# Weight bits routed through PSUM, and a planner that counts a shared port both ways, in a fused attention and feed-forward kernel

## The chip, the cores and the metric

The kernel runs on one core of a Trainium2 chip. The metric is the device time of one execution in microseconds. Five engines matter: TensorE (PE; its weight loads are listed apart as PEld), VectorE (DVE), ScalarE (ACT), GpSimd (POOL), and SyncE (SP), which issues the transfers. DVE and ACT reach both memories on the chip, SBUF and PSUM; PE writes to PSUM; POOL works in SBUF in this kernel.

## The reference

Attention over 2 x 8 heads with 1152 keys of 64 elements and queries averaged in pairs (576 of them), and then two feed-forward layers, on the 1152 x 512 result. The weights come as 64-bit floats.

```python
def _attn_ref(q, k, v):
    B, H, S, D = q.shape                       # 2, 8, 1152, 64
    q_pool = q.reshape(B, H, S // 2, 2, D).mean(axis=3)
    scores = (1 / np.sqrt(D)) * np.matmul(q_pool, k.transpose(0, 1, 3, 2))
    scores = scores - np.max(scores, axis=-1, keepdims=True)
    attn = np.exp(scores)
    attn = attn / (np.sum(attn, axis=-1, keepdims=True) + 1e-09)
    return np.matmul(attn, v)

def _moe_ref(x, w_in, w_out):                  # 1152 x 512, d_ff 2048
    h = x @ w_in
    g = np.where(h >= 1, h, np.where(h <= -1, 0.0, (h + 1) ** 2 / 4))
    return g @ w_out

def _moe2_ref(x, w_in, w_out):
    h = x @ w_in
    return (h / (1.0 + np.exp(-h))) @ w_out
```

## The kernel before

**Arithmetic.** Every operand of a large matmul is split into a high part in a short format (fp32r) and a low part, the rest. `lo_of` (line 135) computes the low part on POOL, in a few places on DVE. A product is then two or three matmuls.

**Attention.** The 16 heads run one after the other and overlap. `inputs(h)` loads q, k and v, splits and transposes k (`khl`, evacuated to `kk` at line 459) and q (`split_q` at line 470, evacuated to `qm` at lines 484 and 488). `scores(h, t)` multiplies a tile of 128 queries with the keys into three banks, which DVE evacuates with their least value (line 562); ACT takes the exponential (line 575). `values(h)` transposes the result in nine chunks (line 610), evacuates each into the two parts `thl` (`split`: either ACT at 588 and DVE at 589, or ACT at 593 and POOL at 594 and 135), and multiplies with v (line 618). The last 64 queries of two heads are done together in `tails`: DVE adds the halves into `ztail` (line 666), multiplies it with the inverse sums (line 670), and PE transposes it into place (line 675). `finish` scales the rows of a pair of heads (line 720).

**Feed-forward layers.** Each layer has four groups of 512 hidden columns, numbered 0 to 7 over both. A step is one group, one of three blocks of 384 tokens and one of four slices of 128 hidden columns: `gemm1` (line 155), the activation (168 to 184), `gemm2` (200, 202), and `keep` (212, 214), which adds to the sum in SBUF.

**Weights.** A group has two kinds of weights, w_in ("i") and w_out ("o"), each in four quarters. A quarter is loaded as 64-bit words (line 97) and made into 32-bit floats by `weight_tasks`: `size` takes the absolute value of the upper words on ACT (102), then four steps on DVE, `clamp` (105), `shift` (109), `sign` (113) and `rest` (117), each with 128 x 512 elements in SBUF, of which `sign` and `rest` read two tensors. ACT then writes the high part (125) and POOL the low part (135). Group 0 is done during attention, its w_in spread over the heads, its w_out after the last heads have been prepared; groups 1 to 7 are done from the opening of the feed-forward stage on (`weights`).

**PSUM.** Of the eight banks, six ("b") rotate over the scores, the transposes and, later, the sums of the layers; two ("y") hold the product with v. A bank is free again when the last step that names it is done.

**Order.** Nothing is scheduled by hand. Every step is an `Op` with a target time, the engines it may run on, the time that it occupies the engine and the time until its result is there, the steps it follows, and the buffers it uses. `plan_out` simulates the engines: again and again it takes the step that can start first, and among equals the one with the least target. The resulting order is the order of each engine's queue; on the chip an engine takes its queue in order and waits for semaphores. A step marked `both` is one that, on DVE, needs the port to SBUF that DVE and POOL share; the plan starts it only when no POOL step is running:

```python
if o.both and e == "DVE" and pool_until[0] <= s < pool_until[1]:
    s = pool_until[1]
...
if e == "POOL":
    pool_until = (s, s + lat)
```

Marked so are the four DVE steps of every weight quarter, the scaling of `ztail`, the scaling in `finish` where it falls on DVE, and the preparation of heads 0 and 1, which may run on DVE or on POOL (`first`).

Of the kernel before, what the change touches and what calls it, by code (L numbers as in the profile page):

```python
# [10 lines left out]
U32 = mybir.dt.uint32  # L11
AF = mybir.ActivationFunctionType
ALU = mybir.AluOpType
# [5 lines left out]
def fused_kernel(  # L19
# [11 lines left out]
    nc = tc.nc  # L31
# [16 lines left out]
    RAWS = 4  # L48
# [13 lines left out]
    LEAST = 2.0**-15  # L62
# [14 lines left out]
    def weight_tasks(idx, kind, pools, RAWS):  # L77
# [6 lines left out]
        def quarter(c):  # L84
# [19 lines left out]
            def clamp():  # L104
                nc.vector.tensor_scalar(st["w"], st["w"], LEAST, MOST, ALU.max, ALU.min)

            def shift():
                wi = st["w"].bitcast(U32)
                nc.vector.tensor_scalar(wi, wi, 3, 0x3FFFFFF8, ALU.logical_shift_left, ALU.bitwise_and)

            def sign():
                wi = st["w"].bitcast(U32)
                nc.vector.scalar_tensor_tensor(wi, st["top"], 0xC0000000, wi, ALU.bitwise_and, ALU.bitwise_or)  # L113

            def rest():
                wi = st["w"].bitcast(U32)
                nc.vector.scalar_tensor_tensor(wi, st["low"], 29, wi, ALU.logical_shift_right, ALU.bitwise_or)
# [144 lines left out]
    def plan_out():  # L262
# [21 lines left out]
        while len(made) < len(ops):  # L284
            best = None
            for e in engines:
                found = []
                for o, k, t in ready[e].values():
                    s = max(t, free[e])
                    for b in o.bufs:  # L290
                        if b.slot is None:
                            have = open_slots[b.group]
                            if b.want is not None:
                                have = [x for x in have if x[1] == b.want]
                            if not have:
                                s = None
                                break
                            s = max(s, min(have)[0] + (0.06 if e == "PE" else 0.04))
                    if s is None:
                        continue  # L300
                    if o.both and e == "DVE" and pool_until[0] <= s < pool_until[1]:
                        s = pool_until[1]
                    found.append((s, o.target, o, k))
# [13 lines left out]
            if e == "POOL":  # L317
                pool_until = (s, s + lat)
            made.append(o)
# [19 lines left out]
    with ExitStack() as at, ExitStack() as keys, ExitStack() as prep:  # L339
# [60 lines left out]
        def inputs(h):  # L400
# [33 lines left out]
            for part in [slice(3 * g, 3 * g + 3) for g in range(3)] if h == 0 else [slice(0, KC)] * 1:  # L434
# [5 lines left out]
                if first:  # L440
                    ways.insert(0, ("DVE", 0.1 + 0.6 * n, 0.18 + 0.6 * n, lo(nc.vector)))
                klo.append(op(t1 + 0.01, ways, [khi[-1]], [kr, kb], both=first))
# [31 lines left out]
            if first:  # L474
                ways.insert(0, ("DVE", 0.6, 0.69, lambda: split_q(nc.vector)))
            sq = op(t3, ways, [lq], [qr, qb], both=first)
# [157 lines left out]
        def tails(h):  # L634
# [35 lines left out]
            o2 = op(t1 + 0.4, ("DVE", 0.2, 0.28, lambda: nc.vector.tensor_scalar_mul(ztail, ztail, sums[key])), [o1, o_inv[key]], [zb], both=True)  # L670
# [98 lines left out]

        STAGES = (("ACT", 0.57, 0.672), ("DVE", 0.332, 0.42), ("DVE", 0.335, 0.427), ("DVE", 0.6, 0.69), ("DVE", 0.6, 0.69))  # L770
        w_last = [None]

        def weights(w, kind, times, deps):


            def get(n, m):
                if (w, kind) not in wsets:
# [4 lines left out]
                    wsets[w, kind] = weight_tasks(w, kind, pools, 1 if (w, kind) == (0, "i") else RAWS)  # L782
# [4 lines left out]
            made = []  # L787
            for n, t in enumerate(times):
                bufs = [Buf("w" if (w, kind) == (0, "i") else "raw"), *whole]
                prev = op(t - 5, ("SP", 2.0, 4.4, lambda n=n: get(n, 0)()), [*deps, w_last[0]], bufs)  # L790
                w_last[0] = prev
                for m, (e, occ, lat) in enumerate(STAGES):
                    prev = op(t + 0.3 * m, (e, occ, lat, lambda n=n, m=m: get(n, m + 1)()), [prev], bufs, both=e == "DVE")
# [114 lines left out]
```

## Time and profile before

| | us |
|---|---|
| median of 3 runs | 695.96 |
| lowest and highest of them | 695.18, 696.70 |
| the profiled execution, its own time | 693.9 |
| its span, first to last instruction | 692.1 |
| TensorE busy | 678.8 |
| VectorE busy | 547.1 |
| GpSimd busy | 431.2 |
| ScalarE busy | 413.7 |

The span is what the rows of the trace add up to; the profiled execution's own time is 1.8 us longer, and the median lies 2.1 us above that. The granted clock of TensorE is 1.00 of full speed in all stretches of the attention and feed-forward stages. A busy PE in this page is one whose pipeline holds a matmul: the rows of neighbouring matmuls overlap, so a stop shows as a gap between rows that is shorter than the time lost. The attention stage ends at about 290 us.

### The profile page before, as it was taken

The numbers are of one execution on the slowest core, as the hardware profiler recorded it, in microseconds if no ns is written. First come the engines' busy times: TensorE is split into PE (matmuls) and PEld (weight loads), VectorE is DVE, ScalarE is ACT, GpSimd is POOL, SyncE is SP. The second block draws the span as 40 slices with busy tenths as digits, with TensorE's granted clock in tenths as the row PEclk, the third lists the DMA queues.
The fourth block names the chain that finished last, engine by engine and source line by source line (L and its number), as shares of the span: only waits on it lengthen the run. The fifth ranks groups of instructions, "written<-read, shape, count | busy, mean of one in ns | idle before, by whom it ended". The sixth has DMA issues, their size and how long they took to land.

```text
span 692.1 us, 11265 instructions
## 1 busy us (share of the span) xinstructions
PE 678.8 (98%) x3959; PEld 627.4 (91%) x3959; DVE 547.1 (79%) x1205; ACT 413.7 (60%) x773; POOL 431.2 (62%) x406
## 2 busy tenths in 40 slices
PE   8999999999999998999999999999999999999997
PEld 6898989888989997899999999999898999999896
DVE  7889989898888889658999796897884894993223
ACT  7988997968797887545544444454554543442221
POOL 7959897969796757735654455478664554453221
PEclk9999999999999999999999999999999999999999
DMA  7332231222110032102332232122131221200012
GB/s 210 109 92 59 92 112 38 79 72 65 50 49 11 26 124 76 62 31 92 122 123 91 92 106 79 61 92 92 62 121 62 92 93 60 93 30 1 1 45 92
DMA packets 28489, 52.93 MB, mean 76 GB/s; under 512 B 4752, under 2 KB 13968, under 8 KB 28432
## 3 DMA queue, kind: packets, MB, share of 16 engines
q1 hardware_dynamic: 28432, 52.21, 23.6%
q8 instruction: 31, 0.51, 0.3%
q14 instruction: 26, 0.21, 0.1%
HBM read 49.81 MB, written 2.39 MB: 75 GB/s over the span
## 4 chain that ended last, share of the span: by engine, by line
PE 81%; DVE 8%; POOL 7%; issue 2%; ACT 1%; DMA 0%; SPq 0%; POOLq 0%; DVEq 0%; ACTq 0%
PE bank L155 27%; PE bank L200 14%; PE bank L202 14%; PE bank L555 9%; PE bank L618 7%; PE bank L610 6%; DVE p L562 2%; POOL thl L135 2%; PE bank L656 2%; POOL xl L135 1%; POOL thl L594 1%; DVE thl L589 1%; PE bank L454 1%; PE bank L647 1%; DVE wf L113 1%
## 5 line engine op out<-in xcount | busy, mean ns | idle before, releaser
L135 POOL TENSOR_TENSOR gl<-gf,gh 128x384 fp32r<-128x384 f32 x96 | 112.4, 1171 | 119.2 <-ACT gh L184 117.5
L155 PE MATMUL bank<-xh,whi 128*128 128x384 f32 x384 | 129.2, 337 | 0.0
L155 PE MATMUL bank<-xl,whi 128*128 128x384 f32 x384 | 129.2, 336 | 0.0
L155 PE MATMUL bank<-xh,wli 128*128 128x384 f32 x384 | 128.9, 336 | 0.0
L562 DVE TENSOR_SCALAR_CACHE_REDUCE p<-bank 128x384 f32<-128x384 f32 x192 | 101.3, 550 | 18.8 <-PE bank L555 17.5
L618 PE MATMUL bank<-thl,vhl 128*128 128x512 f32 x288 | 112.4, 433 | 2.8 <-DVE thl L589 1.5
L178 DVE TENSOR_TENSOR gf<-bank,gf 128x384 f32<-128x384 f32 x96 | 52.9, 551 | 61.6 <-ACT gf L170 57.7
L555 PE MATMUL bank<-kk,qm 128*128 128x384 f32 x384 | 95.3, 352 | 1.9 <-DVE thl L589 1.7
L610 PE MATMUL bank<-ident,p 128*128 128x128 f32 x576 | 85.3, 273 | 0.0
L135 POOL TENSOR_TENSOR thl<-pf,thl 128x512 fp32r<-128x512 f32 x64 | 83.1, 1298 | 3.3
L575 ACT ACTIVATE p<-p,low 128x1152 f32<-128x1152 f32 x64 | 81.0, 1266 | 5.7 <-DVE low L572 5.5
L184 ACT CAST gh<-gf 128x384 fp32r<-128x384 f32 x96 | 49.4, 514 | 53.1 <-DVE gf L178 52.0
L113 DVE SCALAR_TENSOR_TENSOR wf<-wr,wf 128x512 uint32<-128x512 uint32 x64 | 76.2, 1191 | 1.2
L610 PEld LDWEIGHTS bank<-ident,p 128*128 128x128 f32 x576 | 69.4, 140 | 7.8 <-DVE thl L589 0.3
L555 PEld LDWEIGHTS bank<-kk,qm 128*128 128x128 f32 x384 | 65.4, 189 | 10.7 <-DVE thl L589 3.3
L155 PEld LDWEIGHTS bank<-xl,whi 128*128 128x128 f32 x384 | 72.1, 188 | 2.1
L155 PEld LDWEIGHTS bank<-xh,whi 128*128 128x128 f32 x384 | 72.1, 188 | 2.0
L155 PEld LDWEIGHTS bank<-xh,wli 128*128 128x128 f32 x384 | 72.1, 188 | 0.0
L589 DVE TENSOR_TENSOR thl<-bank,thl 128x512 fp32r<-128x512 f32 (+1 forms) x104 | 66.8, 653 | 3.6 <-ACT thl L588 3.3
L588 ACT CAST thl<-bank 128x512 fp32r<-128x512 f32 (+1 forms) x104 | 57.1, 562 | 20.6 <-PE bank L610 16.7
L170 ACT ACTIVATE gf<-bank 128x384 f32<-128x384 f32 x48 | 23.6, 492 | 76.5 <-PE bank L155 73.2
L135 POOL TENSOR_TENSOR wli<-wf,whi 128x512 fp32r<-128x512 f32 x32 | 43.1, 1347 | 41.7 <-ACT whi L125 41.5
(90 smaller groups left out, 1537.7 us busy)
## 6 DMA issues: line engine op xcount, KB each, us to landing
wr<-in_moe_w_in_dram SPq DMA_DIRECT2D x32, 512.0 KB, 3.7
wr<-in_moe_w_out_dram SPq DMA_DIRECT2D x32, 512.0 KB, 3.3
kraw<-in_k_dram SPq DMA_DIRECT2D x16, 288.0 KB, 2.9
vraw<-in_v_dram SPq DMA_DIRECT2D x16, 288.0 KB, 2.8
qraw<-in_q_dram SPq DMA_DIRECT2D x16, 256.0 KB, 3.0
out_dram<-part SPq DMA_DIRECT2D x9, 256.0 KB, 2.0
rb<-row SPq DMA_DIRECT2D x16, 128.0 KB, 3.3
qtraw<-in_q_dram SPq DMA_DIRECT2D x16, 32.0 KB, 2.5
```

The costliest lines, as they stand in the source:

```text
L113: nc.vector.scalar_tensor_tensor(wi, st["top"], 0xC0000000, wi, ALU.bitwise_and, ALU.bitwise_or)
L135: eng.tensor_sub(out, whole, hi.bitcast(F32))
L155: nc.tensor.matmul(ps, lhsT=w[:, c, j * P : (j + 1) * P], rhs=a[:, c, ts_], start=(c == 0 and n == 0), stop=(c == ND - 1 and n == 2),)
L200: nc.tensor.matmul(ps[:, :TB], lhsT=w[:, j, m * P : (m + 1) * P], rhs=a, start=start, stop=stop)
L202: nc.tensor.matmul(ps, lhsT=a[:, m * P : (m + 1) * P], rhs=w[:, j, :], start=start, stop=stop)
L555: nc.tensor.matmul(ps, lhsT=qq[:, c0 : c0 + P], rhs=rhs, start=n == 0, stop=n == last)
L562: nc.vector.tensor_scalar(dst, ps, -1.0, None, ALU.mult, ALU.min, accum_out=mxs[key, t][:, j : j + 1])
L575: nc.scalar.activation(pt(), pt(), AF.Exp, bias=lows[key][:, tt : tt + 1], scale=-1.0, accum_out=sums[key][:, tt : tt + 1])
L588: o1 = op(target, ("ACT", 0.477 * f, 0.587 * f, lambda: nc.scalar.copy(th(), ps())), deps, [bank, tb])
L589: o2 = op(target + 0.3, ("DVE", 0.6 * f, 0.683 * f, lambda: nc.vector.tensor_sub(tl(), ps(), th().bitcast(F32))), [o1], [bank, tb])
L610: nc.tensor.transpose(banks[bank.slot][:, i * P : (i + 1) * P], ps_[p_of[h, i].slot][:, c * P : (c + 1) * P], ident)
L618: nc.tensor.matmul(banks[6 + yb.slot], lhsT=lhsT, rhs=thls[tb.slot][i], start=not count, stop=len(count) == 2 * KC - 1)
```

## The change

Four edits.

- For group 0 (`w` is 0), both kinds, `clamp` writes into a PSUM bank that the quarter holds (`via`), `shift` and `sign` work in that bank, and `rest` reads it and writes SBUF again. These four steps get the costs of `FAR`, 0.6 us each, are no longer marked `both`, and name one of the rotating banks. Groups 1 to 7 are done as before.
- The plan's rule for the port gets a margin of 0.1 us, and a second side: a marked step that starts on DVE keeps POOL from starting until 0.1 us before its end.
- The preparation of head 1 (low part of k, sum of q) may run on POOL alone; head 0 keeps both ways.
- `ztail` is scaled by ACT instead of DVE.

```diff
-    def weight_tasks(idx, kind, pools, RAWS):
+    def weight_tasks(idx, kind, pools, RAWS, via):
...
             def clamp():
-                nc.vector.tensor_scalar(st["w"], st["w"], LEAST, MOST, ALU.max, ALU.min)
+
+                st["x"] = via[c]() if c in via else st["w"]
+                nc.vector.tensor_scalar(st["x"], st["w"], LEAST, MOST, ALU.max, ALU.min)
 
             def shift():
-                wi = st["w"].bitcast(U32)
-                nc.vector.tensor_scalar(wi, wi, 3, 0x3FFFFFF8, ALU.logical_shift_left, ALU.bitwise_and)
+                xi = st["x"].bitcast(U32)
+                nc.vector.tensor_scalar(xi, xi, 3, 0x3FFFFFF8, ALU.logical_shift_left, ALU.bitwise_and)
 
             def sign():
-                wi = st["w"].bitcast(U32)
-                nc.vector.scalar_tensor_tensor(wi, st["top"], 0xC0000000, wi, ALU.bitwise_and, ALU.bitwise_or)
+                xi = st["x"].bitcast(U32)
+                nc.vector.scalar_tensor_tensor(xi, st["top"], 0xC0000000, xi, ALU.bitwise_and, ALU.bitwise_or)
 
             def rest():
-                wi = st["w"].bitcast(U32)
-                nc.vector.scalar_tensor_tensor(wi, st["low"], 29, wi, ALU.logical_shift_right, ALU.bitwise_or)
+                wi, xi = st["w"].bitcast(U32), st["x"].bitcast(U32)
+                nc.vector.scalar_tensor_tensor(wi, st["low"], 29, xi, ALU.logical_shift_right, ALU.bitwise_or)
...
-                    if o.both and e == "DVE" and pool_until[0] <= s < pool_until[1]:
+                    if o.both and e == "DVE" and pool_until[0] - 0.1 <= s < pool_until[1]:
                         s = pool_until[1]
...
             if e == "POOL":
                 pool_until = (s, s + lat)
+            elif o.both and e == "DVE":
+                free["POOL"] = max(free["POOL"], s + lat - 0.1)
...
-                if first:
+                if not h:
                     ways.insert(0, ("DVE", 0.1 + 0.6 * n, 0.18 + 0.6 * n, lo(nc.vector)))
-                klo.append(op(t1 + 0.01, ways, [khi[-1]], [kr, kb], both=first))
+                klo.append(op(t1 + 0.01, ways, [khi[-1]], [kr, kb], both=not h))
...
-            if first:
+            if not h:
                 ways.insert(0, ("DVE", 0.6, 0.69, lambda: split_q(nc.vector)))
-            sq = op(t3, ways, [lq], [qr, qb], both=first)
+            sq = op(t3, ways, [lq], [qr, qb], both=not h)
...
-            o2 = op(t1 + 0.4, ("DVE", 0.2, 0.28, lambda: nc.vector.tensor_scalar_mul(ztail, ztail, sums[key])), [o1, o_inv[key]], [zb], both=True)
+            o2 = op(t1 + 0.4, ("ACT", 0.17, 0.28, lambda: nc.scalar.mul(ztail, ztail, sums[key])), [o1, o_inv[key]], [zb])
...
+        FAR = (("ACT", 0.57, 0.672), *[("DVE", 0.6, 0.69)] * 4)
         STAGES = (("ACT", 0.57, 0.672), ("DVE", 0.332, 0.42), ("DVE", 0.335, 0.427), ("DVE", 0.6, 0.69), ("DVE", 0.6, 0.69))
...
             for n, t in enumerate(times):
                 bufs = [Buf("w" if (w, kind) == (0, "i") else "raw"), *whole]
+                bank = Buf("b")
+                if not w:
+                    via[n] = lambda bank=bank: banks[bank.slot]
                 prev = op(t - 5, ("SP", 2.0, 4.4, lambda n=n: get(n, 0)()), [*deps, w_last[0]], bufs)
                 w_last[0] = prev
-                for m, (e, occ, lat) in enumerate(STAGES):
-                    prev = op(t + 0.3 * m, (e, occ, lat, lambda n=n, m=m: get(n, m + 1)()), [prev], bufs, both=e == "DVE")
+                for m, (e, occ, lat) in enumerate(STAGES if w else FAR):
+                    more = bufs if w or not m else [*bufs, bank]
+                    prev = op(t + 0.3 * m, (e, occ, lat, lambda n=n, m=m: get(n, m + 1)()), [prev], more, both=e == "DVE" and w > 0)
```

## Rows read from the trace of the kernel before

**Rows 1.** Head of the page: span; busy time, share of the span, instructions.

```profile
span 692.1 us, 11265 instructions
PE 678.8 (98%) x3959; PEld 627.4 (91%) x3959; DVE 547.1 (79%) x1205; ACT 413.7 (60%) x773; POOL 431.2 (62%) x406
```

**Rows 2.** Busy us by stretch: PE, PEld, DVE, ACT, POOL; then clock, DMA share, GB/s.

```profile
160.00:250.00 90.00, 90.00 (x616) 82.52 (x615) 76.12 (x253) 76.02 (x138) 69.24 (x74) 1.00 0.18 49
250.00:291.00 41.00, 37.86 (x232) 33.69 (x231) 36.14 (x85) 28.89 (x54) 31.24 (x30) 1.00 0.27 84
```

**Rows 3.** Waits of PEld, 50 to 160 us: us in total, times, longest us.

```profile
PEld bank L555 <- DVE thl L589: 2.5, 2, 2.2
PEld bank L618 <- POOL thl L594: 2.2, 7, 0.5
...
PEld bank L454 <- DVE p L562: 1.1, 2, 0.9
```

**Rows 4.** Waits of PEld, 160 to 250 us, the only kind listed.

```profile
PEld bank L555 <- DVE thl L589: 0.9, 2, 0.4
```

**Rows 5.** Timeline, PE: start, us, what; in brackets PE's idle time before it.

```profile
148.92 0.45 PE L454 MATMUL bank<-ident_r,khl 128*128 128x128 f32 x3 [0.70 <-DVE p L562]
...
159.22 0.62 PE L555 MATMUL bank<-kk,qm 128*128 128x384 f32 x2 [1.72 <-DVE thl L589]
...
261.28 0.98 PE L555 MATMUL bank<-kk,qt 128*128 128x384 f32 x4 [0.58 <-DVE low L572]
...
266.97 0.43 PE L675 MATMUL bank<-jtail,ztail 128*128 128x64 f32 x2 [0.60 <-DVE ztail L670]
...
273.41 0.50 PE L618 MATMUL bank<-thl,vhl 128*128 128x512 f32 x1 [0.76 <-DVE thl L589]
```

**Rows 6.** Timeline, DVE and one of POOL, before those stops.

```profile
143.91 0.53 DVE L105 TENSOR_SCALAR wf<-wf 128x512 f32<-128x512 f32 x1
...
146.60 1.79 DVE L113 SCALAR_TENSOR_TENSOR wf<-wr,wf 128x512 uint32<-128x512 uint32 x1
...
156.47 1.54 POOL L720 TENSOR_TENSOR y<-y,rb 128x512 f32<-128x512 f32 x1 [0.18 <-DVE y L629]
156.49 2.07 DVE L117 SCALAR_TENSOR_TENSOR wf<-wr,wf 128x512 uint32<-128x512 uint32 x1
...
258.97 1.65 DVE L113 SCALAR_TENSOR_TENSOR wf<-wr,wf 128x512 uint32<-128x512 uint32 x1
...
265.57 1.34 DVE L670 TENSOR_SCALAR ztail<-ztail,sum 128x128 f32<-128x128 f32 x1
...
270.99 1.76 DVE L117 SCALAR_TENSOR_TENSOR wf<-wr,wf 128x512 uint32<-128x512 uint32 x1
```

**Rows 7.** Tile wf: ns min/median/max, first and last start in us, forms.

```profile
L105 DVE TENSOR_SCALAR wf<-wf x64: 394/422/1515, 58.5 to 620.6; 128x512 f32<-128x512 f32 x64
L109 DVE TENSOR_SCALAR wf<-wf x64: 409/590/1499, 62.6 to 621.0; 128x512 uint32<-128x512 uint32 x64
L113 DVE SCALAR_TENSOR_TENSOR wf<-wr,wf x64: 672/1344/1833, 64.3 to 621.8; 128x512 uint32<-128x512 uint32 x64
L117 DVE SCALAR_TENSOR_TENSOR wf<-wr,wf x64: 673/694/2070, 73.1 to 623.2; 128x512 uint32<-128x512 uint32 x64
```

**Rows 8.** Groups by form: count, busy us, mean ns of one, idle before.

```profile
L589 DVE TENSOR_TENSOR thl<-bank,thl 128x512 fp32r<-128x512 f32 x96 | 65.2, 684 | 3.6 <-ACT thl L588 3.3
...
L521 ACT ACTIVATE qt<-bank 128x128 fp32r<-128x128 f32 x8 | 2.2, 278 | 0.0
```

**Rows 9.** Waits of PEld, 300 to 690 us, both kinds listed.

```profile
PEld bank L200 <- DVE part L214: 1.3, 2, 1.1
PEld bank L202 <- POOL gl L135: 1.0, 1, 1.0
```

**Rows 10.** Timeline, POOL, at the start: the second head's q and k.

```profile
6.74 1.29 POOL L470 TENSOR_TENSOR qs<-qraw 128x512 f32<-128x512 f32 x1 [0.67 <-DMA qraw<-in_q_dram]
...
8.39 1.44 POOL L135 TENSOR_TENSOR khl<-kraw,khl 128x576 fp32r<-128x576 f32 x1
```

More of the change, by code (lines that the diff above doesn't have):

```diff
@@ L781, in get @@
                         pools = (nat, wpre) if kind == "i" else late_raws()
-                    wsets[w, kind] = weight_tasks(w, kind, pools, 1 if (w, kind) == (0, "i") else RAWS)
+                    wsets[w, kind] = weight_tasks(w, kind, pools, 1 if (w, kind) == (0, "i") else RAWS, via)
                 return wsets[w, kind][n][m]
@@ L786, in weights @@
             whole = [Buf("w" + kind)] if w else []
-            made = []
+            made, via = [], {}
             for n, t in enumerate(times):
                 bufs = [Buf("w" if (w, kind) == (0, "i") else "raw"), *whole]
+                bank = Buf("b")
+                if not w:
+                    via[n] = lambda bank=bank: banks[bank.slot]
                 prev = op(t - 5, ("SP", 2.0, 4.4, lambda n=n: get(n, 0)()), [*deps, w_last[0]], bufs)
                 w_last[0] = prev
-                for m, (e, occ, lat) in enumerate(STAGES):
-                    prev = op(t + 0.3 * m, (e, occ, lat, lambda n=n, m=m: get(n, m + 1)()), [prev], bufs, both=e == "DVE")
+                for m, (e, occ, lat) in enumerate(STAGES if w else FAR):
+                    more = bufs if w or not m else [*bufs, bank]
+                    prev = op(t + 0.3 * m, (e, occ, lat, lambda n=n, m=m: get(n, m + 1)()), [prev], more, both=e == "DVE" and w > 0)
                 prev = op(t + 2, ("ACT", 0.51, 0.61, lambda n=n: get(n, 7)()), [prev], bufs)
```

## The prediction
> **What bounds the kernel now.** I read the page first. TensorE (PE) is busy for 678.8 of 692.1 us [rows 1], so another engine costs time only where it makes PE stop, and the question is not how long VectorE (DVE) and GpSimd (POOL) work but which PE stops they cause. The sums by stretch come next: from 160 to 250 us, where no weight is converted, PE is busy for all of 90.00 us while DVE is busy for 76.12 of them; from 250 to 291 us, where the four quarters of the first w_out group are converted, PE is busy for 37.86 of 41.00 [rows 2]. The waits of the weight loads, which show a stop of PE a little earlier than its matmuls do, say the same: between 50 and 160 us, the stretch of the four quarters of the first w_in group, the three largest kinds shown sum to 2.5 + 2.2 + 1.1 = 5.8 us [rows 3]; the 90 us without weights have 0.9 us [rows 4]. So the first weight group is what makes the attention stage stop.
>
> The timeline shows how. Five stops of PE, 0.70, 1.72, 0.58, 0.60 and 0.76 us, sum to 4.36 us [rows 5]. Just before each stands one DVE instruction that reads and writes SBUF only and takes far longer than its kind can: L113 1.79 us, L117 2.07, L113 1.65, the scaling of ztail at L670 1.34, L117 1.76 [rows 6]. The shortest of the kind are 672 ns for L113 and 673 for L117 [rows 7]. The clearest case is at 156.49 us: L720 on POOL started 0.02 us earlier and ended at 158.01; L117 ended at 158.56 [rows 6], so it got about 0.55 us of work done after POOL had let go. Behind it on DVE stood the evacuation L589, and PE waited for that. The instructions of DVE with a PSUM operand are not held up this way: L589, 96 of them with POOL busy for most of the stage, means 684 ns [rows 8], against 672 for the undisturbed L113.
>
> **The change, part by part.**
>
> *Weight bits through PSUM.* In 8 quarters the four DVE steps get a PSUM operand, so each has at most one SBUF operand. What goes: the excess of the four L113 and L117 above is 1.79 - 0.67 = 1.12, 2.07 - 0.67 = 1.40, 1.65 - 0.67 = 0.98 and 1.76 - 0.67 = 1.09 us. A stop can't give back more than the excess that made it, so 0.70 + 1.40 + 0.58 + 0.76 = 3.4 us come back.
>
> What it adds on DVE: clamp and shift run at 394 and 409 ns at their shortest [rows 7]. Neither SBUF to PSUM nor PSUM to PSUM is in the trace. The ends are their present shortest time and the 684 ns of L589 [rows 8]; I take 684, the nearest row with a PSUM operand of 512 columns. That is 0.29 + 0.275 us more, and 0.01 for each of the other two: 0.58 us for a quarter, 4.7 us for eight. I cost it at nothing: DVE idles for 13.9 of 90 us in the stretch without weights [rows 2], and the excess removed is larger than what is added. If that cover is gone it is 4.7 us.
>
> [...]
>
> What it adds as a wait: clamp now waits for a free bank, and from clamp to the last step one of the six rotating banks is taken from PE. Behind a waiting clamp on DVE stand the evacuations L562 and L589, and PE waits for those. The four steps of the fourth quarter now stretch from 143.91 to 158.56 us, 14.7 us [rows 6]; a bank would be held as long if they stay as spread. What a bank less costs no row shows. Lower end 0 (a bank taken away can't help); upper end one stop for each quarter like the longest in the stretch without weights, 0.4 us [rows 4]: 3.2 us. I take 0.1 for each, 0.8 us, since that stretch runs with two waits in 90 us and so has room.
>
> *ztail scaled by ScalarE (ACT).* Eight instructions leave DVE. The held one cost the stop of 0.60 us [rows 5] out of an excess of 1.34 - 0.28 = 1.06, so 0.60 us comes back. On ACT it should take 278 ns, as L521 of 128x128 does [rows 8], 2.2 us in all; ACT is busy 76.02 of 90 us [rows 2], which covers it. It waits there for the sum's inverse and for L666; behind it stand an exponential or an evacuation, and PE waits for that. Price if the cover fails: 0.28 us each, 2.2 us.
>
> *POOL's side.* A POOL instruction also waits where DVE came first. The waits for L594 are 2.2 us, seven of them [rows 3]. Between 0 and 2.2 I take 0.5, since most are short and a matmul in flight hides part of each.
>
> *Second head on POOL alone.* Its split of q and low part of k already run on POOL, at 6.74 and 8.39 us [rows 10]. Taking DVE's way from them changes no step that was chosen: nothing, with the start of the kernel as it is.
>
> *The plan counts the port both ways.* The plan gives the order on each engine and nothing else; it is no wait on the chip. In attention, hardly any DVE step is left that is marked as needing the port: those of head 0 and the scaling in `finish`, where that falls on DVE. So the new rule acts mainly from 300 us on, on the weights of groups 1 to 7. There two kinds of waits of PE's weight loads are listed, 1.3 us for L214 and 1.0 for POOL's gl [rows 9]. A better order removes them (-2.3), a worse one doubles them (+2.3); nothing chooses between the two, so I take 0 and keep both for the range. From the first ztail on, every later choice of the plan may also fall otherwise; I put no sign to that.
>
> Sum: -3.4 - 0.6 - 0.5 + 0.8 = -3.7 us. The profiled execution took 693.9 us, 1.8 beyond its span; it would take 690.2. The median of the runs shown is 695.96, 2.1 higher; the same 3.7 us less makes 692.3.
>
> **The rivals.**
>
> A, the freed time is used up: the two slower steps and the bank leave DVE as late as before at half of the stops. For it: DVE idles for only 4.9 of 41 us from 250 to 291 [rows 2], and four quarters come close together there. Against it: the held time removed is larger than what is added. Half of 4.0 comes back, the bank costs 0.8: -1.2, 694.8 us.
>
> B, slower: banks run short. Each quarter keeps a bank for as long as its steps are spread, and PE, which runs ahead of DVE only as far as it has banks, stops once for each quarter by the mean of today's stops, 4.36 / 5 = 0.87 us: 8 x 0.87 = 7.0, less the 4.5 won, +2.5: 698.5 us. It decides from 4.5 / 8 = 0.56 us for each quarter. For it: 14.7 us of holding, and up to four quarters close together after 250 us, where the first steps of the feed-forward layer hold banks as well. Against it: the nearly stopless 90 us.
>
> C, the change doesn't do what it says: the forms that no row shows, SBUF to PSUM and PSUM to PSUM, are held by POOL all the same. Then only ztail's 0.6 comes back against 0.8 for the banks: 696.2 us. Against it: of the forms with PSUM that are there, none is held [rows 8].
>
> D, the reordered feed-forward layers win too: -3.7 - 2.3, 690.0 us.
>
> **How the numbers follow.** Forecast 0.52, A 0.19, B 0.16, C 0.05, D 0.08. The forecast's 692.3 is the likeliest and the number given. 0.2% is 1.4 us, about what a measurement of this kernel can tell from no change. Faster by more: the forecast and D, 0.60. Within: A and C, 0.24. Slower: B, 0.16. The range goes from 687.5 (4.0 back, with all of 2.2 and 2.3 on top: 8.5 less) to 697.5 (4.0 back, but 3.2 for the banks and 2.3 for the order: 1.5 more); it leaves out B, 0.16.
>
> **What would show it.** In the trace after: the four steps of the first eight quarters all near 0.68 us, whatever POOL does, and all of L562 and L589 behind them on time; PE idle before 250 us near what the 90 us without weights have; ztail on ACT at about 0.28 us; the second head's two POOL steps at 6.7 and 8.4 us as now; the weights of groups 1 to 7 still held at times. I am wrong if the steps are held in PSUM too (C), if weight loads wait for banks that a weight quarter holds (B), if PE stops behind DVE in new places of the same size (A), or if the stretch from 300 us on gains or loses more than 2.3 us.

## The result, and the profile after

The changed kernel takes 689.02 us (median of 4 runs, 688.70 to 689.87) against 695.73 for the kernel before beside it (4 runs, 695.18 to 696.70): 0.9904 of it, interval 0.9887 to 0.9921. It is 6.7 us faster; the forecast was 3.7 us and its range held the time. Profiled execution against profiled execution it is 693.9 to 689.0, 4.9 us; the other 1.8 us lie between the profiled executions and the medians (below, the clock). In the code all lines from the edit on stand 2 to 4 lines lower: `clamp`, `shift`, `sign`, `rest` are L107, L111, L115, L119; the evacuations L562 and L589 are now L566 and L593; the transposes L610 are L614, the product with v L618 is L622, and the ztail scaling L670 is L674.

The page of the kernel after, its head:

```profile
span 687.1 us, 11298 instructions
...
PE 678.8 (99%) x3959; PEld 627.0 (91%) x3959; DVE 524.7 (76%) x1191; ACT 418.0 (61%) x787; POOL 424.8 (62%) x406
```

Against [rows 1], TensorE (PE) has the same 678.8 us of work in a span that is 5.0 us shorter, and VectorE (DVE) is busy 22 us less although in eight quarters `clamp` and `shift` now take 687 and 695 ns (groups by form below) against 394 and 409 at their shortest [rows 7].

Busy time by stretch, after (columns as in [rows 2]; behind PE the number of its matmuls):

```profile
50.00:160.00 110.00, 109.87 (x737) 99.02 (x736) 98.62 (x314) 100.83 (x191) 95.39 (x98) 1.00 0.29 78
160.00:250.00 90.00, 89.96 (x609) 81.43 (x607) 73.05 (x240) 76.33 (x142) 65.30 (x70) 1.00 0.14 43
250.00:291.00 41.00, 39.10 (x233) 33.69 (x232) 31.28 (x77) 28.18 (x54) 27.45 (x29) 1.00 0.25 84
300.00:480.00 180.00, 179.96 (x1024) 179.64 (x1024) 153.43 (x243) 87.19 (x166) 103.80 (x83) 1.00 0.28 94
```

The matmul counts say roughly where the time came from, since both kernels issue the same 3959. Before, the four stretches held 704, 616, 232 and 1019. From 50 to 160 us there are 33 more, at 110 / 737 = 0.149 us each 4.9 us. From 160 to 250 there are 7 fewer (-1.0 us, in part because other kinds of matmuls now lie there), from 250 to 291 one more, and from 300 to 480 five more, at 180 / 1024 each 0.9 us.

Counts mix matmuls of several lengths. The start of one and the same step in both kernels is free of that: the last transpose of k (second number of "5.3 to 245.8"), the 25th matmul of its kind in the first layer, and the first matmul of the second layer's `gemm2`, each before and after:

```profile
L454 PE MATMUL bank<-ident_r,khl x144: 222/234/306, 5.3 to 245.8; 128*128 128x128 f32 x144
L458 PE MATMUL bank<-ident_r,khl x144: 221/230/305, 5.4 to 242.1; 128*128 128x128 f32 x144
...
303.44 0.34 PE L155 MATMUL bank<-xh,whi 128*128 128x384 f32 x1
299.28 0.34 PE L157 MATMUL bank<-xh,whi 128*128 128x384 f32 x1
...
L202 PE MATMUL bank<-who,gh x144: 392/398/400, 492.4 to 687.6; 128*128 128x512 f32 x144
L204 PE MATMUL bank<-who,gh x144: 392/398/400, 487.3 to 682.6; 128*128 128x512 f32 x144
```

The changed kernel is 0.3 us behind at 38 us (first product of the tails), 3.7 us ahead at the last transpose of k, 4.2 ahead at about 300 us and 5.0 ahead in the second layer. So the w_in quarters gave 4.0 us, the w_out stretch 0.5 and what follows 0.8. The w_out quarters, where three of the five marked stops of [rows 5] stood, gave little.

Waits of PE's weight loads after, 50 to 160 us, the largest three (us in total, times, longest):

```profile
PEld bank L614 <- DVE p L566: 0.5, 2, 0.3
PEld bank L622 <- POOL thl L137: 0.4, 2, 0.2
PEld bank L559 <- DVE thl L593: 0.3, 1, 0.3
```

and from 250 to 292 us:

```profile
PEld bank L559 <- DVE p L566: 1.7, 3, 0.8
PEld bank L614 <- DVE wf L119: 1.3, 1, 1.3
PEld bank L614 <- DVE p L566: 0.8, 2, 0.5
PEld bank L679 <- ACT ztail L674: 0.6, 1, 0.6
```

The 2.5, 2.2 and 1.1 us of [rows 3] are gone; what is left there is smaller by kind than the 0.9 of [rows 4]. In the w_out stretch most of the old waits were replaced by new ones. One of them is a wait that the kernel before could not have: PE waits for L119, which is the step that gives the quarter's bank back.

Timeline after, DVE and PE (start, us, what; in brackets the idle time):

```profile
249.14 0.67 DVE L107 TENSOR_SCALAR bank<-wf 128x512 f32<-128x512 f32 x1
...
252.82 0.69 DVE L119 SCALAR_TENSOR_TENSOR wf<-wr,bank 128x512 uint32<-128x512 uint32 x1
...
253.56 0.66 PE L614 MATMUL bank<-ident,p 128*128 128x128 f32 x4 [0.85 <-DVE wf L119]
```

The bank was held from 249.14 to 253.51 us. PE's next transposes waited for it and stopped 0.85 us.

Groups by form after, whole span (count, busy us, mean ns of one, idle before):

```profile
L107 DVE TENSOR_SCALAR bank<-wf 128x512 f32<-128x512 f32 x8 | 5.5, 687 | 0.3 <-ACT wf L102 0.3
...
L111 DVE TENSOR_SCALAR bank<-bank 128x512 uint32<-128x512 uint32 x8 | 5.6, 695 | 0.0
...
L115 DVE SCALAR_TENSOR_TENSOR bank<-wr,bank 128x512 uint32<-128x512 uint32 x8 | 5.5, 691 | 0.0
...
L119 DVE SCALAR_TENSOR_TENSOR wf<-wr,bank 128x512 uint32<-128x512 uint32 x8 | 5.5, 683 | 0.1
...
L115 DVE SCALAR_TENSOR_TENSOR wf<-wr,wf 128x512 uint32<-128x512 uint32 x56 | 64.5, 1152 | 1.1
...
L674 ACT ACTIVATE ztail<-ztail,sum 128x128 f32<-128x128 f32 x8 | 3.2, 395 | 0.3 <-DVE ztail L670 0.3
```

The 32 steps of the first group have a mean of 683 to 695 ns, none over 697, with POOL busy for 95.39 of 110 us in the w_in stretch; the 56 `sign` steps of groups 1 to 7, which kept SBUF on both sides, still have a mean of 1152 against 672 undisturbed [rows 7].

### The profile page after: what moved, and what is told of

Its sections match the earlier page's. It is cut to its first block, busy times and chain, and to the rows that moved or that the text cites. A ratio compares the mean times of both kernels' runs of the same rounds, so it can differ in the third digit from the quotient of the medians.

```text
span 687.1 us, 11298 instructions
## 1 busy us (share of the span) xinstructions
PE 678.8 (99%) x3959; PEld 627.0 (91%) x3959; DVE 524.7 (76%) x1191; ACT 418.0 (61%) x787; POOL 424.8 (62%) x406
## 4 chain that ended last, share of the span: by engine, by line
PE 93%; DVE 4%; POOL 2%; issue 1%; ACT 0%; POOLq 0%; ACTq 0%
PE bank L157 28%; PE bank L202 14%; PE bank L204 14%; PE bank L559 12%; PE bank L622 9%; PE bank L614 9%; PE bank L660 2%; PE bank L458 1%; PE bank L651 1%; DVE p L566 1%; PE bank L485 1%; POOL xl L137 1%; PE bank L394 0%; POOL wli L137 0%; POOL gl L137 0%
## 5 line engine op out<-in xcount | busy, mean ns | idle before, releaser
L137 POOL TENSOR_TENSOR gl<-gf,gh 128x384 fp32r<-128x384 f32 x96 | 109.7, 1144 | 120.6 <-ACT gh L186 115.8
L566 DVE TENSOR_SCALAR_CACHE_REDUCE p<-bank 128x384 f32<-128x384 f32 x192 | 101.9, 550 | 19.7 <-PE bank L559 16.4
L622 PE MATMUL bank<-thl,vhl 128*128 128x512 f32 x288 | 113.5, 434 | 0.0
L614 PE MATMUL bank<-ident,p 128*128 128x128 f32 x576 | 85.5, 274 | 1.1 <-DVE wf L119 0.8
L614 PEld LDWEIGHTS bank<-ident,p 128*128 128x128 f32 x576 | 69.1, 140 | 10.9 <-DVE p L566 1.4
L593 DVE TENSOR_TENSOR thl<-bank,thl 128x512 fp32r<-128x512 f32 (+1 forms) x104 | 66.9, 654 | 5.4 <-ACT thl L592 5.0
L137 POOL TENSOR_TENSOR wlo<-wf,who 128x512 fp32r<-128x512 f32 x32 | 46.0, 1436 | 37.8 <-ACT who L127 37.8
L115 DVE SCALAR_TENSOR_TENSOR wf<-wr,wf 128x512 uint32<-128x512 uint32 x56 | 64.5, 1152 | 1.1
```

The costliest lines, as they stand in the source:

```text
L115: nc.vector.scalar_tensor_tensor(xi, st["top"], 0xC0000000, xi, ALU.bitwise_and, ALU.bitwise_or)
L137: eng.tensor_sub(out, whole, hi.bitcast(F32))
L566: nc.vector.tensor_scalar(dst, ps, -1.0, None, ALU.mult, ALU.min, accum_out=mxs[key, t][:, j : j + 1])
L593: o2 = op(target + 0.3, ("DVE", 0.6 * f, 0.683 * f, lambda: nc.vector.tensor_sub(tl(), ps(), th().bitcast(F32))), [o1], [bank, tb])
L614: nc.tensor.transpose(banks[bank.slot][:, i * P : (i + 1) * P], ps_[p_of[h, i].slot][:, c * P : (c + 1) * P], ident)
L622: nc.tensor.matmul(banks[6 + yb.slot], lhsT=lhsT, rhs=thls[tb.slot][i], start=not count, stop=len(count) == 2 * KC - 1)
```

## Experiments

Two theories stood at the start. Theory 1: the steps in PSUM are what wins, since POOL doesn't hold them there (none over 697 ns). Theory 2: the kernel before has an unlucky order, and any edit that makes the planner choose anew would win about as much. Labels with a_ are edits of the changed kernel, those with b_ of the kernel before; diffs are against the one or the other. Ratios are to the kernel before, measured again beside each group of runs (medians 695.31, 695.25 and 695.36 us).

### The same order with the steps in SBUF

```diff
-                st["x"] = via[c]() if c in via else st["w"]
+                st["x"] = st["w"]
```

The bank is still reserved and the costs are unchanged, so the order on every engine is that of the changed kernel, line for line; only the operands of the 32 steps differ.

> The changed kernel with one line undone: the four DVE steps of group 0 work in SBUF again, in place. The plan is as in the changed kernel, so every engine has exactly the same queue; only the operands differ. Theory 1, the shared port: the steps are held by POOL again (some at 1.0 to 2.0 us instead of 0.69), and since the plan no longer keeps them away from POOL's steps, at least as many stops come back as before: 694 to 698 us. Theory 2, the new order: the gain of 6.7 us comes from other places in the queues; the time stays within 1 us of the changed kernel, 688 to 690 us, and the steps are even shorter in clamp and shift (0.4 us).

Measured: 696.27 us, 1.0016 (1.0006 to 1.0026); 7.25 us more than the changed kernel (7.6 by the spans of the profiled executions, 694.7 against 687.1). Busy time by stretch, this run:

```profile
50.00:160.00 110.00, 106.74 (x710) 95.15 (x709) 100.28 (x300) 97.22 (x184) 94.58 (x93) 1.00 0.28 75
...
250.00:291.00 41.00, 37.06 (x219) 30.98 (x218) 34.04 (x81) 28.36 (x53) 29.27 (x29) 1.00 0.25 85
```

It has 27 matmuls fewer in the first stretch and 14 fewer in the second. As the queues are the same, the start of every matmul can be compared: this run is 0.1 us behind the changed kernel at 60 us, 4.2 us from 113 to 247 us, and 7.6 us from 279 us to the end. So 4.1 us are lost at the w_in quarters and 3.4 at the w_out quarters. Its groups by form, DVE, 50 to 200 us, and two rows of its timeline:

```profile
L115 DVE SCALAR_TENSOR_TENSOR wf<-wr,wf 128x512 uint32<-128x512 uint32 x4 | 5.2, 1293 | 0.0
L119 DVE SCALAR_TENSOR_TENSOR wf<-wr,wf 128x512 uint32<-128x512 uint32 x4 | 4.6, 1138 | 0.0
L111 DVE TENSOR_SCALAR wf<-wf 128x512 uint32<-128x512 uint32 x4 | 3.7, 924 | 0.0
L107 DVE TENSOR_SCALAR wf<-wf 128x512 f32<-128x512 f32 x4 | 3.2, 793 | 0.3 <-ACT wf L102 0.3
```

```profile
114.41 1.79 DVE L115 SCALAR_TENSOR_TENSOR wf<-wr,wf 128x512 uint32<-128x512 uint32 x1
...
116.86 0.66 PE L614 MATMUL bank<-ident,p 128*128 128x128 f32 x4 [1.28 <-DVE thl L593]
```

This is the cleanest of the runs: with the order fixed, the operands alone are worth 7.25 us. Theory 1 holds for this order. It also shows that the w_out quarters do gain from PSUM, 3.4 us, against the same order in SBUF; against the kernel before, whose order is another, the stretch gained 0.5. But the order was planned for steps that POOL doesn't hold (683 to 695 ns in PSUM, 793 to 1293 in SBUF at the w_in quarters). So 7.25 us is what the operands are worth in this order; an order planned for steps in SBUF is another matter (below, other orders).

### The other edits, one undone at a time

ztail back on DVE:

```diff
-            o2 = op(t1 + 0.4, ("ACT", 0.17, 0.28, lambda: nc.scalar.mul(ztail, ztail, sums[key])), [o1, o_inv[key]], [zb])
+            o2 = op(t1 + 0.4, ("DVE", 0.2, 0.28, lambda: nc.vector.tensor_scalar_mul(ztail, ztail, sums[key])), [o1, o_inv[key]], [zb], both=True)
```

> The changed kernel with ztail scaled by DVE again, marked as needing the port. My sum: one stop of 0.6 us comes back in eight scalings: 689.5 to 690 us. Rival: the order is so sensitive that any such edit moves the time by 1 to 3 us either way: outside 688 to 691 us.

Measured: 690.39 us, 0.9932 (0.9918 to 0.9945), 1.4 us above the changed kernel, a little more than the sum expected and inside 688 to 691, so not what the rival said. The order changes with the edit too, so 1.4 is the worth of the edit with its order.

The plan's rule taken out, margin and second side:

```diff
-                    if o.both and e == "DVE" and pool_until[0] - 0.1 <= s < pool_until[1]:
+                    if o.both and e == "DVE" and pool_until[0] <= s < pool_until[1]:
...
-            elif o.both and e == "DVE":
-                free["POOL"] = max(free["POOL"], s + lat - 0.1)
```

> The changed kernel without the plan's two-sided rule for the port (margin and second side taken out). Theory 1, the shared port in attention: the rule has nearly nothing to decide before 300 us, so the first 290 us keep their gain of about 4 us; from 300 us on the stop of about 1 us at step L200 may come back: 689 to 691 us. Theory 2, the order: without the rule most of the gain is lost: 693 us or more.

Measured: 694.71 us, 1.0001 (0.9990 to 1.0011), as the second theory had it: no gain is left, with all 32 steps still free. Its trace says why. Groups by form, the scaling in `finish`, and the timeline of the first place:

```profile
L722 POOL TENSOR_TENSOR y<-y,rb 128x512 f32<-128x512 f32 x4 | 6.3, 1572 | 0.0
...
L722 DVE TENSOR_TENSOR y<-y,rb 128x512 f32<-128x512 f32 x4 | 5.1, 1271 | 0.0
```

```profile
53.04 1.34 DVE L722 TENSOR_TENSOR y<-y,rb 128x512 f32<-128x512 f32 x1
...
53.36 1.49 POOL L596 CAST thl<-pf 128x512 fp32r<-128x512 f32 x1
...
54.91 0.50 PE L620 MATMUL bank<-thl,vhl 128*128 128x512 f32 x1 [1.09 <-POOL thl L596]
```

The changed kernel and the one before put seven of the eight scalings on POOL and one on DVE. Without the rule DVE takes four. In the first place POOL's cast L596, started 0.32 us behind, needs 1.49 us (its shortest here is 0.61), and PE waits for it. The pair of stops of 1.09 and 0.29 us behind L596 stands three times, at 55, 157 and 192 us, 4.1 us in all. The next run keeps the rule out and ties the scaling to POOL, the last pair excepted:

```diff
-            ways = [("POOL", 1.27, 1.32, lambda: scale(nc.gpsimd)), ("DVE", 1.0, 1.09, lambda: scale(nc.vector))]
+            ways = [("POOL", 1.27, 1.32, lambda: scale(nc.gpsimd))]
+            if h == NH - 1:
+                ways.append(("DVE", 1.0, 1.09, lambda: scale(nc.vector)))
```

> The changed kernel without the plan's two-sided rule, but the scaling in finish may run on DVE for the last pair of heads alone. In the run without the rule that scaling went to DVE four times instead of once, at 1.27 us, held POOL's cast (1.49 us instead of 0.61) and PE stopped behind it three times for 1.3 and 0.45 us. Theory 1: the rule's whole worth before 300 us is that it keeps this scaling on POOL: 688.5 to 690.5 us. Theory 2: the rule also orders other steps that matter: 692 us or more.

Measured: 689.25 us, 0.9914 (0.9901 to 0.9926), as the first theory had it. Up to 306 us every engine has the queue of the changed kernel. So beside PSUM the rule is worth 5.7 us (694.71 against 689.02), and 5.5 of them are this choice of an engine; the 0.2 left is less than the runs can tell.

The second head's edit needed no run: with both ways given back to head 1, the planner makes the same queues on all engines, line for line. It is worth nothing, as forecast.

### PSUM for w_in alone

```diff
+            near = (w, kind) == (0, "i")
...
-                for m, (e, occ, lat) in enumerate(STAGES if w else FAR):
-                    more = bufs if w or not m else [*bufs, bank]
+                for m, (e, occ, lat) in enumerate(FAR if near else STAGES):
+                    more = [*bufs, bank] if near and m else bufs
```

The w_out quarters go back to SBUF, marked `both` again, and hold no bank.

> The changed kernel with PSUM for w_in of group 0 alone; the w_out steps of group 0 run in SBUF and are marked for the port as before. If the banks cost what the stop of 1.0 us at 252 us and the smaller ones behind it suggest, and the held steps of w_out cost 0.6 + 0.8 us as before: about even, 688 to 690 us. If the w_out quarters gain nothing from PSUM, since their four banks and their crowding cost as much: below 688 us. If they gain as much as w_in: 691 us or more.

Measured: 686.90 us, 0.9881 (0.9864 to 0.9898), the fastest run of the study, and below 688 as expected for the case that the w_out quarters gain nothing from PSUM. Its interval overlaps that of the changed kernel; by the medians it is 2.1 us faster. Its second stretch:

```profile
250.00:291.00 41.00, 40.09 (x246) 36.66 (x245) 32.02 (x73) 27.05 (x53) 32.45 (x29) 1.00 0.26 84
```

13 matmuls more than the changed kernel has there, 13 x 41 / 246 = 2.2 us: about all of the difference. To ask whether the bank is the reason, the w_out steps stay in SBUF but reserve a bank that they don't use:

```diff
-                    more = [*bufs, bank] if near and m else bufs
+                    more = [*bufs, bank] if not w and m else bufs
```

> The kernel with PSUM for w_in alone, in which each w_out quarter also takes a rotating bank from its second to its fifth step, in the plan, without using it: PE has one bank less for that time, and the steps run in SBUF as before. If the bank taken from PE is what the w_out quarters lost by going through PSUM: 688.5 to 690 us, with stops of 0.5 to 1 us between 250 and 270 us. If what they lost is DVE's time and their crowding instead: within 0.7 us of 686.9.

Measured: 692.76 us, 0.9963 (0.9952 to 0.9975), 5.9 us slower than without the reservation and well above what either theory expected. Busy time of the same stretch, its longest wait of PE there, and the step before it:

```profile
250.00:291.00 41.00, 37.33 (x221) 32.14 (x220) 34.50 (x77) 27.63 (x53) 29.66 (x28) 1.00 0.27 84
```

```profile
PE bank L157 <- DVE thl L593: 1.6, 1, 1.6
```

```profile
268.62 1.50 DVE L107 TENSOR_SCALAR wf<-wf 128x512 f32<-128x512 f32 x1
```

25 matmuls fewer than in the run before, 4.2 us. But the bank isn't alone at work: the order moved with it, and the 16 w_out steps are now held 5.9 us in all against 3.5 us (durations less the shortest of each in [rows 7]); the stop of 1.6 us stands behind a `clamp` that took 1.50 us, against 394 ns at its shortest [rows 7]. What the runs show is that a reservation here costs, with the order it forces, up to 5.9 us. How much of this is the bank by itself stays open.

### The kernel before, in other orders

Six runs leave all steps in SBUF. Two carry the rule, two carry half of it each, and two touch nothing that has to do with the port. The expectations stand in this order: `a_nopsum`, `b_plan`, `b_margin`, `b_second`, `b_slack`, `b_period`.

```diff
# b_plan: margin and second side of the rule, as in the change
# a_nopsum: the same, and ztail on ACT (the changed kernel without its PSUM form)
# b_margin: the margin alone
-                    if o.both and e == "DVE" and pool_until[0] <= s < pool_until[1]:
+                    if o.both and e == "DVE" and pool_until[0] - 0.1 <= s < pool_until[1]:
# b_second: the second side alone
+            elif o.both and e == "DVE":
+                free["POOL"] = max(free["POOL"], s + lat - 0.1)
# b_slack: the plan's allowance for a semaphore
-    SLACK = 0.2
+    SLACK = 0.21
# b_period: the spacing of the heads' target times
-    PERIOD = 15.8
+    PERIOD = 15.75
```

> The changed kernel without PSUM: the first group's steps stay in SBUF and are marked for the port as before; the plan's two-sided rule and ztail on ACT are in. Theory 1: only steps without a need of the port run undisturbed beside POOL; w_in's stops of 0.7 + 1.7 us and the smaller ones come back: 690 to 693 us. Theory 2: a plan that counts the port both ways keeps such steps out of each other's way by itself, in attention too: 686 to 688 us, as with PSUM for w_in alone.

> The kernel before with the plan's two-sided rule alone. Theory 1, the rule alone does nothing for DVE steps that start late on the chip: the stops behind L113, L117 and L670 stay: 694 to 697 us. Theory 2, the rule by itself removes most collisions: 688 to 691 us, with the one step of ztail still held once or twice.

> The kernel before with the margin of 0.1 us alone: a marked DVE step isn't started within 0.1 us before a POOL step that is already placed. The step at 156.49 us that lost 1.4 us to a POOL step 0.02 us earlier is such a case, but the plan had put the DVE step and the POOL step side by side for lack of the other side of the rule. If the margin is what counts: 687 to 691 us. If the other side is: 694 to 697 us.

> The kernel before with the second side of the rule alone (a marked DVE step keeps POOL from starting), without the margin of 0.1 us. If this side is what the rule alone won: 687 to 690 us. If the margin did it: 694 us or more.

> The kernel before with one planning number moved from 0.2 to 0.21 us (SLACK, the time that the plan adds for a handing over). Nothing in it concerns the port; the plan comes out in another order in a good part of the queues. Theory 1, the rule matters: the collisions stay and so does the time, 694 to 697 us. Theory 2, chance of the order: any new order moves the time by several us, and it lands anywhere from 687 to 699 us.

> The kernel before with the target times of the heads set 15.75 us apart instead of 15.8 (PERIOD): a second new order without any rule for the port changed. Theory 1: 694 to 697 us. Theory 2: anywhere from 687 to 699 us, and not where the run with SLACK 0.21 lies.

Held is what the 16 w_in steps took beyond 8.6 us, which is four times the shortest of each in [rows 7]; it is the sum of the four groups by form from 50 to 200 us, as shown for the SBUF run above (`a_sbuf` in the table, 16.7 - 8.6 = 8.1). In the changed kernel (`after`) the steps take 0.67 to 0.70 us each by themselves, and none is held. Intervals of the ratio are 95%.

| run | us | ratio (interval) | held, us | matmuls 50 to 160 |
|---|---|---|---|---|
| before | 695.3 | 1 | 7.8 | 704 |
| a_sbuf | 696.27 | 1.0016 (1.0006 to 1.0026) | 8.1 | 710 |
| b_slack | 696.83 | 1.0015 (1.0004 to 1.0026) | 7.8 | 698 |
| b_second | 696.05 | 1.0013 (1.0001 to 1.0025) | 8.5 | 701 |
| b_margin | 690.94 | 0.9937 (0.9921 to 0.9952) | 5.3 | 728 |
| b_period | 689.98 | 0.9923 (0.9906 to 0.9940) | 5.9 | 721 |
| a_nopsum | 688.67 | 0.9907 (0.9893 to 0.9921) | 3.4 | 729 |
| b_plan | 688.30 | 0.9905 (0.9891 to 0.9920) | 5.3 | 737 |
| after | 689.02 | 0.9904 (0.9887 to 0.9921) | 0 | 737 |

Without the PSUM form the time is 688.67 us, between what the two theories expected and nearer to the second, and the rule alone, 688.30, does as well, as its second theory had it. The margin alone, 690.94, and the second side alone, 696.05, both came out as expected for the case that the margin counts. Theory 2 of the start is half right. The period, which says nothing of the port, won 5.4 us by a new order; the allowance, as neutral, won nothing. And the plan's rule by itself reaches the time of the whole change, in much the same place: by the start of the same steps it is 3.8 us ahead of the kernel before at the last transpose of k and 5.3 at 300 us, the changed kernel 3.7 and 4.2, PSUM for w_in alone 4.2 and 7.1. The gains don't add: what the bank form removes at the w_in quarters, a good order in SBUF removes as well. With the rule and the scaling of `ztail` on ACT in both, PSUM for all eight quarters is worth nothing that the runs can tell (689.02 against 688.67), and PSUM for w_in alone 1.8 us (686.90), with intervals that overlap. In the table the runs near 696 have 7.8 us and more of held time in the w_in steps, and those from 688 to 691 have 3.4 to 5.9; this sorting was found after the runs and no run was made to test it. Whether the rule finds good orders or had the luck that the period had can't be told from one order each: its two halves came out at 696.05 and 690.94 apart, 688.30 together. What can be told is that the eight orders with the steps in SBUF lie anywhere from 688.3 to 696.8. Of the six with the w_in steps in PSUM four lie from 686.9 to 690.4; the other two are the one in which `finish` went to DVE, 694.7, and the one with a bank reserved for w_out in SBUF, 692.8. This division too was made after the runs.

### The clock behind a stop

In the profiles of two of these runs a stop cost more than itself. The second side alone, timeline and busy time by stretch:

```profile
159.38 1.54 POOL L722 TENSOR_TENSOR y<-y,rb 128x512 f32<-128x512 f32 x1 [0.18 <-DVE y L631]
159.40 2.06 DVE L117 SCALAR_TENSOR_TENSOR wf<-wr,wf 128x512 uint32<-128x512 uint32 x1
...
162.12 0.62 PE L557 MATMUL bank<-kk,qm 128*128 128x384 f32 x2 [1.72 <-DVE thl L591]
```

```profile
155.00:163.00 8.00, 6.28 (x46) 5.46 (x44) 7.94 (x23) 6.34 (x12) 5.76 (x6) 1.00 0.11 19
163.00:164.00 1.00, 1.00 (x5) 0.91 (x4) 1.00 (x4) 0.76 (x2) 1.00 (x2) 0.51 0.11 30
164.00:165.00 1.00, 1.00 (x5) 0.91 (x5) 0.82 (x5) 0.39 (x1) 1.00 (x2) 0.50 0.75 224
165.00:166.00 1.00, 1.00 (x6) 1.00 (x5) 1.00 (x3) 0.20 (x1) 0.63 (x1) 0.50 0.03 8
166.00:167.00 1.00, 1.00 (x6) 0.92 (x5) 0.74 (x4) 0.91 (x2) 0.55 (x1) 0.78 0.00 0
```

It is the same stop as in the kernel before, 1.72 us behind a `rest` held by the scaling on POOL [rows 5, 6]. Here the granted clock then fell to 0.50 of full speed while PE was busy throughout, and four matmuls of L557 took 1.49 us (at 163.43 us) against 0.86 for the same four of L555 in the kernel before (at 160.35). The sum of what is missing to 1.00, 0.49 + 0.50 + 0.50 + 0.22 = 1.7 us, is an estimate of what the fall cost. The profile with the allowance changed has two such falls, to 0.50 from 91 to 93 us and from 163 to 165 us, each after stops of about 0.70 and 1.11 us close together. In the profiled execution of the kernel before the clock stayed at 1.00:

```profile
160.00:161.00 1.00, 1.00 (x8) 0.96 (x7) 1.00 (x4) 0.68 (x2) 1.00 (x2) 1.00 0.12 29
...
163.00:164.00 1.00, 1.00 (x9) 0.96 (x8) 1.00 (x5) 0.93 (x2) 1.00 (x2) 1.00 0.00 0
```

So the clock falls after such a stop in one execution and not in another. That is part of the spread of the kernel before, whose 57 executions in these runs take 693.39 to 697.07 us. The 17 whose mean granted clock is 0.996 to 0.998 take 695.31 to 697.07; the 40 at 0.999 and 1.000 take 693.39 to 695.73. The run without the rule splits the same way: 694.49 to 694.76 in nine executions, and 695.96 to 696.21 in the three at 0.998. All four executions of the changed kernel, whose longest stop from 50 to 290 us is 0.85 us, have 0.999 or 1.000, and its median lies on its profiled time, 689.02 and 689.01. But the 40 executions at full clock still spread over 2.3 us, with the profiled 693.9 near the short end; and in the run with the steps in SBUF the clock makes no such split (696.26 to 696.83 at 0.999 and 1.000, 695.97 to 696.59 below). What else moves the times no run shows.

## Why the prediction was right, and where its steps were wrong

**Right.** The sum gave 3.7 us, all of it before 300 us, and by the start of the same steps the changed kernel gained 4.5 us from 38 to 300 us; the other terms that make up the 6.7 us, 0.8 from 300 us on and 1.8 between the profiled executions and the medians, stood at nothing in it (0.3 was lost before 38 us). So the time lies in the range, nearer to rival D's 690.0 than to 692.3, in part by luck: the terms below were wrong in both directions. What bounds the kernel was right: each PE stop behind a held DVE step. The forms with a PSUM operand are free of POOL (rival C falls): all four kinds at 683 to 695 ns, next to the 684 taken, and worth 7.25 us with the order fixed. The 4.7 us more for `clamp` and `shift` cost nothing visible: DVE idles 17 of 90 us in the 160 to 250 stretch, and the w_in stretch has hardly a wait left (rival A falls there). The second head is worth nothing. The weights of groups 1 to 7 are still held.

The POOL side: the waits of the weight loads for L594, 2.2 us [rows 3], came down to 0.2 us for its successor L598. PE's own row for L594 has only 0.4 us before, and there is none after, so the 0.5 taken fits what the rows show of PE's stops. These rows, before and after, and the one after from 300 us on that is named below:

```profile
PE bank L618 <- POOL thl L594: 0.4, 2, 0.2
...
PEld bank L622 <- POOL thl L598: 0.2, 1, 0.2
...
PEld bank L204 <- POOL gl L137: 1.0, 1, 1.0
```

What the traces show of the holding: with an operand in PSUM and at most one input in SBUF the steps took 683 to 695 ns, also beside a POOL step that started 0.15 us earlier (the first two rows, from the changed kernel). `rest` still has two operands in SBUF, an input and its output, not one as forecast, and took 683 ns. With both inputs in SBUF L113 took 1.79 us in the kernel before [rows 6], beside the POOL step of the third row, and L115 1.79 us in the order of the changed kernel (`a_sbuf`). With one input, in SBUF in place, `clamp` and `shift` took up to 1.52 and 1.50 us in the kernel before [rows 7].

```profile
257.77 1.28 POOL L137 TENSOR_TENSOR thl<-pf,thl 128x512 fp32r<-128x512 f32 x1
257.92 0.69 DVE L115 SCALAR_TENSOR_TENSOR bank<-wr,bank 128x512 uint32<-128x512 uint32 x1
...
146.24 1.61 POOL L135 TENSOR_TENSOR khl<-kraw,khl 128x576 fp32r<-128x576 f32 x1
```

Which of the operands decides no run separates; that the two engines share a port to SBUF is the author's reading of these times, which no run tests by itself.

**The PSUM term, -3.4.** Its mechanism was right, its size and place were not. The two marked stops of the w_in stretch, 0.70 and 1.72 us, were counted at 2.1 us after the cap by the held excess; the stretch gave 4.0 us. The many waits below the five marked ones went too, the 2.2 us for L594 among them. The marked stops after 250 us, counted at 1.3 us and with `ztail` at 1.9, gave 0.5 net of the new ones. And the term isn't PSUM's alone: an order by the rule, with the steps in SBUF, gave as much (688.30 us).

**The bank, +0.8.** 0.1 us a quarter fits the w_in quarters, where no wait for a bank's return is listed. For w_out, which had 0.4 us of it, it was too little: one stop of 0.85 us behind L119 alone, and the whole form costs 2.2 us there against w_out in SBUF in its own order. Rival B named this mechanism and this place, four quarters close together after 250 us; it was wrong to price all eight quarters by one figure.

**ztail, -0.6.** On ACT it takes 395 ns, not 278: the row taken for it reads PSUM and multiplies with a constant, while `ztail` lies in SBUF and is multiplied with a column of sums; which of the two makes the difference no run shows. Undone, with the order that follows, it costs 1.4 us. In the new order ACT's scaling itself ends one wait of 0.6 us of the weight loads.

**The rule, 0.** "The new rule acts mainly from 300 us on" was the step that failed outright. It named the scaling in `finish`, "where that falls on DVE", and went past it; in the kernel before that is one of eight. But the planner chose POOL under the old costs and marks; under the new ones, without the rule, it takes DVE four times, and that costs 5.5 us. That in the plan DVE is free earlier because the steps in PSUM no longer wait for POOL is the likely reason, which no run tests. And the rule alone, put at 0, takes the kernel before to 688.30 us, 7 us faster, with the order that it makes. From 300 us on the forecast of little held: the wait for L214, 1.3 us [rows 9], is gone, POOL's wait stays at 1.0, and 0.8 us was won, inside the 2.3 allowed (rival D's place, a third of its size). It is the new order's and not the rule's: the run without the rule and with the scaling tied to POOL has it too (1024 matmuls from 300 to 480 us).

**The order, no sign.** It deserved a size: 689.98 to 696.83 us with the two neutral edits. A range of 10 us about the forecast held the time, but the sum's terms have far less certainty than their two digits show.

**From the profile to the median.** "The same 3.7 us less" assumed that the 2.1 us between the profiled execution and the median are fixed. They aren't: the changed kernel has none of it, and for the kernel before the falls of the clock make up a part of it.

The fastest version found is the w_in quarters through PSUM and w_out in SBUF: 686.90 us.

## What to carry to other kernels

Where one engine holds up another's steps, as POOL did DVE's here (`rest` 2.07 us against 0.67 at its shortest [rows 6, 7]), there are two ways out: take an operand of the shorter work to the other memory, or order the work around it. Here the order by itself reached 688.30 us, and the operand without the rule 689.25, once `finish` was tied to POOL; both together reached 689.02, and 686.90 with the operand moved at the w_in quarters alone. The operand in PSUM was worth most where the order wasn't made for steps in SBUF (7.25 us with the order held fixed); an order was worth anything from nothing to 7 us. Move the operand where PE has banks to spare, as at the w_in quarters (no wait for a bank's return is listed there), and not where the stages overlap and the bank is missed, as at w_out (PE stopped 0.85 us for it). Before an edit of a planner is credited with a gain, run a reorder that has nothing to do with it, and look at which engine each step with a choice ends up on.

## What the runs showed of the hardware

- After a stop of 1.72 us, with PE busy again, the granted clock was 0.50 to 0.78 of full speed from 163 to 167 us in the run with the second side alone, at an estimated cost of 1.7 us (the sum of what is missing to 1.00); after stops of 0.70 and 1.11 us close together it fell to 0.50 twice in the run with the allowance changed. After the same 1.72 us in the profiled execution of the kernel before it stayed at 1.00.
- Holding goes both ways: `rest` on DVE took 2.07 us (0.67 at its shortest) behind a scaling on POOL that started 0.02 us earlier [rows 6, 7], and POOL's cast of 128x512 took 1.49 us (0.61 at its shortest there) behind a scaling on DVE that started 0.32 us earlier, in the run without the rule.
- DVE from SBUF to PSUM (687 ns), within PSUM (695, 691) and from PSUM to SBUF (683) costs nearly the same at 128x512 in 32 bits; only the one-input steps lose by it (394 and 409 ns in SBUF).
- ACT scales 128x128 by a column within SBUF in 395 ns.
